# Seven block products for K and V of six token tiles, in a linear attention block with a gated FFN

## The chip, the cores and the metric

The kernel runs on one core of one Trainium2 chip. The metric is the device time of one execution in microseconds (us); before the change the median of three runs is 758.9 us (758.7 to 759.54). The engines have their own in-order instruction queues and wait for each other on semaphores: PE (TensorE, matrix products into PSUM), DVE (VectorE), ACT (ScalarE), POOL (GpSimd) and SP, which here issues most DMAs.

## The reference, cut to what matters

```python
def phi(t): return jnp.where(t > 0, t + 1, jnp.exp(t)) + 1e-6

xn = layernorm(x)                     # x: 2048 tokens x 1024
q, k, v = split(xn @ wqkv)            # 32 heads of 32
pq, pk = phi(q), phi(k)
kv = einsum("bhsd,bhse->bhde", pk, v) # sum over all tokens
z  = einsum("bhsd->bhd", pk)
num, den = pq @ kv, pq . z + 1e-6
s = (num / den) @ wo
g = silu((silu(xn @ w_gate) * (xn @ w_up)) @ w_down)   # width 3584
out = x + s * g
```

All tensors are bfloat16; the normalised tokens are kept in float16.

## The kernel before, in words

The kernel has three stages. The first makes the normalised, transposed tokens, K and V, the sum kv and most of Q; the second makes the attention output s; the third is the FFN with the final combination. The change is in the first two. Their order on PE, DVE, ACT and POOL is written out by hand (FRONT_ORDER): an engine executes what the program emits for it in just that order.

**Tiles and blocks.** The 2048 tokens are 16 tiles of 128, and 4 blocks of 4 tiles. xnT holds the transposed tokens in two tensors of 1024 tokens (pass 0: blocks 0 and 1; pass 1: blocks 2 and 3). Tiles 0 to 7 are normalised one by one and transposed on PE. Blocks 2 and 3 go another way: statistics on DVE (L322, L335), three small Newton steps on POOL for the reciprocal root (L362 to L366), the norm on DVE (emit_norm, L371) into a piece of ws_all, and emit_xT_block: a DMA to DRAM (L415) and a transposing DMA back into xnT (L416), both on SP's queue.

**A K/V tile directly.** emit_B(i, c) computes one of four column chunks of 512 of a token tile: 8 matmuls of 512 columns over the 1024 input features (L428). For the two chunks of K, ACT evaluates exp and relu out of PSUM (L186, L187), and after the second chunk DVE makes phi from them in two operations (L190, L191). The two chunks of V are copied to v_sb by ACT (L446). emit_C(i) then adds the tile's outer products of phi(K) and V into three PSUM tiles kvz (8 matmuls of 129 columns, L457); it needs both copies of V.

**Q by seven block products.** A QGroup computes 256 columns of Q for 1024 tokens as a 2 x 2 block product with seven products instead of eight (a Strassen-Winograd form). Its operands are sums of blocks of xnT (xsum_ops, L138: five operations of 128x2048 per pass) and of the weights (wsum_ops, L152 to L155: four operations per group of 256 columns). Each product is 4 matmuls of 512 columns, so a group has 28 instead of 32. Part a makes two products into accumulators X and Y, ACT copies X to SBUF (L228), DVE adds Y (L231). Part b makes a product into Z, DVE adds it (L236), then one more product each on top of X and Y, which gives two of the four blocks, evaluated by ACT. Part c makes the last two products on top of X and Y; DVE subtracts them from the sum (L246), and ACT evaluates the result. Part d is phi on DVE (L190, L191) for a row of 1024 tokens.

**The order of the first stage.** After the first tiles, a loop over tiles 4 to 15 emits the four chunks of each tile; from tile 9 on, one of six QGroups is interleaved with each tile. Two more (qa, qb) come in the second stage. Between the chunks, fill(n) takes operations from a list, later: statistics, norms, transposes, then the sums for Q. PSUM has five buffers (psB) for the chunks and for X, Y and Z.

**The second stage.** emit_KVZ masks kvz on DVE. emit_ND makes numerator and denominator of one token tile (8 matmuls, L632) and divides on DVE (L636 to L642); emit_OT sends the tile to DRAM and back transposed; emit_S is one of 32 units of the product with wo (8 matmuls of 512 columns, L669, copied by ACT, L673). nd tiles and units alternate, and the phi rows left over from qa and qb lie between them. After the last nd tile the first weights of the FFN are loaded.

Of the kernel before, what the change touches and what calls it, by code (L numbers as in the profile page):

```python
# [21 lines left out]
def kernel(  # L22
# [171 lines left out]
    wqp = p12.enter_context(tc.tile_pool(name="wqp", bufs=1))  # L194
    phiw = p12.enter_context(tc.tile_pool(name="phiw", bufs=5))
    qtmp = p12.enter_context(tc.tile_pool(name="qtmp", bufs=2))

    wq_sb = wqp.tile([P, DC, D], BF16, name="wq_sb")
    NM_Q = D // FW
    pqT_tiles = {}  # L200

    def exp_tile():
        return phiw.tile([P, SP_TOK], BF16, name="e_t", tag="e_t")

    class QGroup:


        def __init__(self, p, m):
            w = wq_sb[:, :, m * FW:(m + 1) * FW]
            self.lhs, self.rhs = block_operands(w, ws_all[:, m // 2, m % 2]), x_operands(p)  # L210
            self.out = wgu.tile([P, 2, SP_TOK], BF16, name="pqT", tag=("wg_sb" if m % 2 == 0 else "wu_sb"))
            pqT_tiles[(p, m)] = self.out
            self.row = {}
# [35 lines left out]
        def part_d(self, i):  # L249
            emit_phi(self.out[:, i, :], self.row[i][:])  # L250

    ET = mybir.EngineType
    FRONT_ORDER = {ET.PE, ET.DVE, ET.Activation, ET.Pool}
    kvz_ps = [psA.tile([P, GPT, NDW], FP32, name=f"kvz{j}", tag="A") for j in range(NJ)]
    with ExitStack() as p1:
# [4 lines left out]
        wkv_sb = wpool.tile([P, DC, 2 * D], BF16, name="wkv_sb")  # L260
        NV = 3
        v_bufs = [wpool.tile([P, G, NDW], BF16, name=f"v_sb{k}") for k in range(NV)]
# [7 lines left out]
        def x_ap(i):  # L270
            return xp_tiles[i // 2][:, i % 2, :]
# [45 lines left out]
        def emit_stats(i, parts=None):  # L317
            if i not in part_stats:
                part_stats[i] = small.tile([P, NSC, nc.vector.BN_STATS_DIM], FP32, name="stats", tag="stats")
            xr = x_ap(i).rearrange("p (c f) -> p c f", f=SCH)  # L320
            for c in (range(NSC) if parts is None else parts):
                nc.vector.bn_stats(out=part_stats[i][:, c, :], in_=xr[:, c, :])  # L322
            if parts is None:
                emit_aggr(i)
# [43 lines left out]
        def emit_norm(i, dst, cols=None):  # L368
# [3 lines left out]
                                           op0=ALU.subtract, op1=ALU.mult)  # L372

# [6 lines left out]
        def xn_blk_slot(b):  # L382
            o = xn_base + (1 - b % 2) * TPB * D
            return ws_flat[:, o:o + TPB * D].rearrange("p (t d) -> p t d", t=TPB).bitcast(FP16)
# [35 lines left out]
        kv_tiles = {}  # L420

        def v_of(i):
            return v_bufs[i % NV]

# [27 lines left out]

        def emit_C(i):
            pk_sb, v_sb = pk_tiles.pop(i), v_of(i)
            for g in range(G):
                j, gi = divmod(g, GPT)
                nc.tensor.matmul(kvz_ps[j][:, gi, 0:P + 1], lhsT=pk_sb[:, g * P:(g + 1) * P],  # L457
                                 rhs=v_sb[:, g, 0:P + 1],
                                 start=(i == 0 and gi == 0), stop=(i == NT - 1),
                                 skip_group_check=True)  # L460
# [10 lines left out]


        later = deque()
        for b in range(2, NB):
            for t in range(TPB):
                later.append(lambda i=b * TPB + t: emit_stats(i, parts=(0,)))
                later.append(lambda i=b * TPB + t: (emit_stats(i, parts=(1,)), emit_aggr(i)))
            later.append(lambda i=b * TPB: emit_rstd(i))
            if b > 2:
                for t in range(TPB):  # L480
                    later.append(lambda b=b, t=t: emit_norm(b * TPB + t, xn_blk_slot(b)[:, t, :]))
                later.append(lambda b=b: emit_xT_block(b))
            else:
                norm_b2 = [lambda b=b, t=t: emit_norm(b * TPB + t, xn_blk_slot(b)[:, t, :]) for t in range(TPB)]
                norm_b2.append(lambda b=b: emit_xT_block(b))

        pos = 2 * TPB + 1 + 4
        later = deque(list(later)[:pos] + norm_b2 + list(later)[pos:])
        later.extend(xsum_ops(0))
        for m in range(NM_Q):  # L490
            later.extend(wsum_ops(wq_sb[:, :, m * FW:(m + 1) * FW], ws_all[:, m // 2, m % 2]))
        later.extend(xsum_ops(1))

        def fill(n):
            for _ in range(min(n, len(later))):
                later.popleft()()

        with tc.manual_schedule(engines=FRONT_ORDER):
# [66 lines left out]

            Q0 = 2 * TPB + 1
            early = deque([(0, m) for m in range(NM_Q)] + [(NPASS - 1, m) for m in range(NM_Q - 2)])
            for i in range(TPB, NT):
                grp = QGroup(*early.popleft()) if i >= Q0 and early else None
                nf = 1 if grp else 2  # L570
                emit_B(i, 0)
                fill(nf)
                emit_C(i - 1)
                if grp:
                    grp.part_a()
                emit_B(i, 1)
                fill(nf)
                if grp:
                    grp.part_b()
                if i == TPB:  # L580
                    emit_T(TPB + 2)
                emit_B(i, 2)
                fill(nf)
                if i == TPB:
                    emit_T(TPB + 3)
                if grp:
                    grp.part_c()
                emit_B(i, 3)
                if grp:
                    grp.part_d(0)  # L590
                    grp.part_d(1)
                fill(nf)
            emit_C(NT - 1)
            assert not later and not early
        gate([x_loads[i] for i in range(first_wave, NT)], marks[("B", 1)], sync=True)
        gate(wq_loads, marks[("B", 3)], sync=True)

    with ExitStack() as p2:
# [90 lines left out]
        with tc.manual_schedule(engines=FRONT_ORDER | {ET.SP}):  # L689

            qa, qb = (QGroup(NPASS - 1, m) for m in (NM_Q - 2, NM_Q - 1))
            for c in range(NCC):
                nc.sync.dma_start(out=wo_sb[:, :, c * CW:(c + 1) * CW], in_=wo_v[:, :, c * CW:(c + 1) * CW])
            emit_KVZ()
            qa.part_a()
            qa.part_b()
            nd_tile()
            qb.part_a()
            emit_OT()
            qa.part_c()  # L700
            nd_tile()
            qa.part_d(0)
            qb.part_b()
            emit_OT()
            nd_tile()
            qb.part_c()
            emit_OT()
            rows = deque(((qa, 1), (qb, 0), (qb, 1)))
            while units:
                if len(units) % 4 != 2:  # L710
                    nd_tile()
                else:
                    for _ in range(min(2, len(rows))):
                        grp, i = rows.popleft()
                        grp.part_d(i)
                if len(units) == 2 * NCC:
                    sum_w(0, 0)
                    sum_w(0, 1)
                s_unit()
                emit_OT()  # L720
    p12.close()
    ps12.close()
# [372 lines left out]
```

## Time and profile before

| what | value |
|---|---|
| median of three runs | 758.9 us |
| the profiled execution | 758.81 us |
| its span, first to last instruction | 757.0 us |
| granted TensorE clock, mean | 0.999 |
| PE busy / DVE / ACT / POOL | 746.9 / 482.1 / 276.5 / 50.9 us |
| K/V matmuls (L428) | 379 ns each in the rows, 24 in a row take 5.18 us |
| first stage ends (last kvz) | at about 166.4 us |
| second stage ends (first FFN matmul) | at 244.09 us |

Matmuls are pipelined, so the duration in a row (379 ns) is longer than the distance between two of them (5.18 / 24 = 0.216 us). A group of rows gives line, engine, operation, output and inputs with shapes, count, then busy time and mean ns of one, then the idle time of the engine just before and what ended it. A row of the timeline gives start and duration in us; several instructions of one kind are merged. A few records of matmuls are missing from the trace, so counts in a window can be a little low.

### The profile page before, as it was taken

How to read it: one execution, taken by the hardware profiler on the slowest of the kernel's cores; microseconds unless marked ns; L12 is line 12 of the kernel's file. 1: busy time of each engine (PE TensorE's matmuls, PEld its weight loads, DVE VectorE, ACT ScalarE, POOL GpSimd, SP SyncE). 2: the span in 40 equal slices, each digit the busy share in tenths (PEclk: the TensorE clock that was granted, in tenths of full speed). 3: DMA queues.
4: the chain of work that ended last, by engine and by line, in shares of the span. 5: the costliest groups of instructions: out<-in, count | busy, mean ns of one | idle time of the engine just before them, and what ended most of it. 6: DMA issues, size and time to landing. Idle time of an engine off the chain costs nothing.

```text
span 757.0 us, 9915 instructions
## 1 busy us (share of the span) xinstructions
PE 746.9 (99%) x3724; PEld 351.7 (46%) x3764; DVE 482.1 (64%) x897; ACT 276.5 (37%) x482; POOL 50.9 (7%) x112
## 2 busy tenths in 40 slices
PE   8999999999999999999999999999999999999997
PEld 4544444444544444444444444444444444444454
DVE  6686666349843577776787777776755744445453
ACT  4444556555223434343433334343443111111111
POOL 3311000000000000000000000000000112222220
PEclk9999999999999999999999999999999999999999
DMA  9606100016899334573354634543869854554200
GB/s 318 223 16 184 40 1 0 1 45 186 237 234 287 115 102 146 165 217 110 93 174 147 202 107 131 170 150 112 298 225 352 299 181 181 181 178 171 96 29 29
DMA packets 127663, 115.98 MB, mean 153 GB/s; under 512 B 29440, under 2 KB 108416, under 8 KB 126336
## 3 DMA queue, kind: packets, MB, share of 16 engines
q1 hardware_dynamic: 122720, 106.58, 44.8%
q10 hardware_dynamic: 4896, 8.78, 3.5%
q8 instruction: 29, 0.48, 0.3%
q14 instruction: 18, 0.15, 0.1%
HBM read 70.52 MB, written 38.54 MB: 144 GB/s over the span
## 4 chain that ended last, share of the span: by engine, by line
PE 95%; DVE 3%; issue 1%; DMA 0%; ACT 0%; DVEq 0%; ACTq 0%
PE X L131 29%; PE Y L131 28%; PE kv_ps L428 14%; PE Z L131 10%; PE s_ps L669 6%; PE qY L131 3%; PE qX L131 3%; PE kvz L457 1%; PE nd_ps L632 1%; DVE o_sb L642 1%; PE qZ L131 1%; DVE stats L322 0%; PE tr_ps L397 0%; DMA xp<-in_A_x_dram 0%; DVE pqT L191 0%
## 5 line engine op out<-in xcount | busy, mean ns | idle before, releaser
L131 PEld LDWEIGHTS <-ws_all 128*128 128x128 bf16 x1420 | 137.8, 98 | 162.6 <-issue 0.2
L758 DVE TENSOR_TENSOR q<-n,Y 128x512 f32<-128x512 f32 x63 | 43.4, 688 | 116.8 <-PE Y L131 105.8
L428 PE MATMUL kv_ps<-wkv_sb,xnT 128*128 128x512 bf16 x496 | 114.2, 379 | 1.2 <-DVE xnT L411 0.5
L131 PEld LDWEIGHTS <-xs 128*128 128x128 bf16 x616 | 58.0, 98 | 63.1
L1028 POOL TENSOR_TENSOR o_out<-y,xres 128x512 bf16<-128x512 f32 x29 | 33.5, 1157 | 652.4 <-DVE y L1027 652.4
L428 PEld LDWEIGHTS <-xnT 128*128 128x128 f16 x512 | 49.3, 98 | 57.6 <-DVE xnT L411 0.7
L131 PE MATMUL Y<-xs,ws_all 128*128 128x512 f16 (+3 forms) x308 | 70.3, 360 | 0.0
L131 PE MATMUL X<-xnT,ws_all 128*128 128x512 f16 (+1 forms) x278 | 70.1, 379 | 0.2
L131 PE MATMUL Z<-xs,ws_all 128*128 128x512 f16 x224 | 57.5, 379 | 0.0
L131 PE MATMUL Y<-xnT,ws_all 128*128 128x512 f16 x224 | 57.5, 379 | 0.0
L131 PE MATMUL X<-xs,ws_all 128*128 128x512 f16 x224 | 57.5, 379 | 0.0
L882 ACT ACTIVATE g<-cg 128x512 bf16<-128x512 f32 x56 | 35.4, 633 | 53.9 <-DVE cg L773 53.9
L764 DVE TENSOR_TENSOR u<-Z,q 128x512 f32<-128x512 f32 x63 | 43.3, 688 | 16.0 <-PE Z L131 15.9
L882 ACT ACTIVATE g<-X 128x512 bf16<-128x512 f32 x28 | 16.7, 598 | 99.3 <-PE X L131 99.2
L754 ACT COPY n<-X 128x512 f32<-128x512 f32 x63 | 37.0, 587 | 28.2 <-PE X L131 27.8
L907 DVE TENSOR_TENSOR ho<-g,up 128x1024 bf16<-128x1024 bf16 x56 | 38.3, 686 | 0.5
L131 PEld LDWEIGHTS <-wg_sb 128*128 128x128 bf16 x224 | 21.9, 98 | 26.6 <-issue 0.3
L673 ACT CAST s_sb<-s_ps 128x512 bf16<-128x512 f32 x32 | 18.4, 587 | 43.4 <-PE s_ps L669 29.5
L131 PEld LDWEIGHTS <-wu_sb 128*128 128x128 bf16 x224 | 21.9, 98 | 26.4
L1027 DVE TENSOR_TENSOR y<-y,s_in 128x512 f32<-128x512 f32 x31 | 21.3, 686 | 20.2 <-ACT y L1021 15.9
L1021 ACT ACTIVATE y<-X 128x512 f32<-128x512 f32 x8 | 4.8, 598 | 69.7 <-PE X L131 61.2
L186 ACT ACTIVATE e_t<-kv_ps 128x512 bf16<-128x512 f32 x32 | 19.2, 600 | 29.6 <-PE kv_ps L428 27.2
(140 smaller groups left out, 1046.1 us busy)
## 6 DMA issues: line engine op xcount, KB each, us to landing
h_dram<-ho SPq DMA_DIRECT2D x56, 256.0 KB, 2.5
wg_sb<-in_B_w_gate_dram SPq DMA_DIRECT2D x14, 512.0 KB, 4.0
wu_sb<-in_B_w_up_dram SPq DMA_DIRECT2D x14, 512.0 KB, 4.0
wdr<-in_B_w_down_dram SPq DMA_DIRECT2D x14, 512.0 KB, 4.0
ws_all<-h_dram SPq DMA_DIRECT2D x4, 1792.0 KB, 8.3
wds_dram<-wdsA SPq DMA_DIRECT2D x14, 384.0 KB, 2.6
hp_a<-h_dram SPq DMA_DIRECT2D x3, 1792.0 KB, 9.0
o_dram<-o_sb ACTq DMA_DIRECT2D x16, 256.0 KB, 3.1
```

The lines of the kernel that those rows point to most:

```text
L131: marks["mm"] = nc.tensor.matmul(acc[:, 0:c1 - c0], lhsT=lhs(k), rhs=rhs(k)[:, c0:c1], start=(first and k == 0), stop=(k == n - 1), skip_g ...
L186: nc.scalar.activation(out=e, in_=t, func=ACT.Exp)
L428: mm = nc.tensor.matmul(kv_ps[:], lhsT=xn_tok_ap(i)[:, dc, :], rhs=wkv_sb[:, dc, c * CW:(c + 1) * CW], start=(dc == 0), stop=(dc == DC - 1))
L669: mm = nc.tensor.matmul(s_ps[:], lhsT=oT[:, c, ttok], rhs=wo_sb[:, c, cc * CW:(cc + 1) * CW], start=(c == 0), stop=(c == G - 1))
L673: nc.scalar.copy(out=s_sb[:, cc * CW:(cc + 1) * CW], in_=s_ps[:])
L754: nc.scalar.copy(out=n[:], in_=self.X[:])
L758: nc.vector.tensor_tensor(out=self.q[:], in0=n[:], in1=self.Y[:], op=ALU.add)
L764: nc.vector.tensor_tensor(out=self.u[:], in0=Z[:], in1=self.q[:], op=ALU.add)
L882: nc.scalar.activation(out=self.g[:, i, j * TB:(j + 1) * TB], in_=src, func=ACT.Silu)
L907: nc.vector.tensor_tensor(out=self.ho[:, i], in0=self.g[:, i], in1=self.up[:, i], op=ALU.mult)
L1027: nc.vector.tensor_tensor(out=t[:], in0=t[:], in1=self.s_in[:, i, cs], op=ALU.mult)
L1028: (nc.vector if last and (i, j) != (0, 0) else nc.gpsimd).tensor_tensor(out=self.o_out[:, i, cs], in0=t[:], in1=self.xres[:, i, cs], op=AL ...
```

## The change

Tiles 9/13, 10/14 and 11/15 no longer go through emit_B. A new class, KVGroup, computes K (or V) of two tiles that lie 512 tokens apart, for all 1024 columns, with seven block products; its operands on the token side are the sums that Q of pass 1 uses anyway, its operands on the weight side are sums of quarters of the K (or V) weights, five operations of 128x2048 for each of K and V (kv_sum_ops). Three of these sums are stored in places that are free by then (quarters of xnT that no later product reads, and the buffers of the last two pqT tiles); two are written over the weights' own quarters. Tile 12 follows tile 8, then twelve groups of Q, K and V in the order of seq. A group's part c and its phi are emitted after the next group's part a. The norms of blocks 2 and 3 move from DVE to ACT as one operation with a scale and a bias per partition; DVE computes that bias (emit_neg_mr). The first part of qa moves into the first stage; its phi rows and those of qb move to units 3, 5, 7 and 9 of the second stage, the nd tiles are spread to unit 19. There are four v buffers instead of three, four exp tiles instead of five, and the blocks' places in ws_all are exchanged.

```diff
-    phiw = p12.enter_context(tc.tile_pool(name="phiw", bufs=5))
+    phiw = p12.enter_context(tc.tile_pool(name="phiw", bufs=4))
...
+        def emit_neg_mr(i):
+            gid = grp_of[i]
+            mv, rstd, tiles = grp_state[gid]
+            n = len(tiles)
+            neg_mr[gid] = small.tile([P, TPB], FP32, name="nmr", tag="nmr")
+            nc.vector.scalar_tensor_tensor(out=neg_mr[gid][:, 0:n], in0=mv[:, 0:n, 0], scalar=-1.0, in1=rstd[:, 0:n],
+                                           op0=ALU.mult, op1=ALU.mult)
+
+        def emit_norm_act(i, dst):
+            mv, rstd, k = ln_state[i]
+            nc.scalar.activation(out=dst, in_=x_ap(i), func=ACT.Identity, bias=neg_mr[grp_of[i]][:, k:k + 1],
+                                 scale=rstd[:, k:k + 1])
...
+        def kv_sum_ops(which, places):
+            w = wkv_sb[:, :, which * D:(which + 1) * D]
+            w11, w12, w21, w22 = w[:, 0:HD, 0:CW], w[:, 0:HD, CW:D], w[:, HD:DC, 0:CW], w[:, HD:DC, CW:D]
+            s1, s5, s2 = places
...
+            return [lambda: tt(out=s1, in0=w11, in1=w22, op=ALU.add), lambda: tt(out=s5, in0=w11, in1=w21, op=ALU.add),
+                    lambda: tt(out=s2, in0=w12, in1=w22, op=ALU.add),
+                    lambda: tt(out=w21, in0=w22, in1=w21, op=ALU.subtract),
+                    lambda: tt(out=w12, in0=w11, in1=w12, op=ALU.subtract)]
...
+            def part_b(self):
+                Z = psB.tile([P, CW], FP32, name="kZ", tag="B")
+                self.mm(Z, "M1", True)
+                nc.vector.tensor_tensor(out=self.u[:], in0=self.u[:], in1=Z[:], op=ALU.add)
+                self.mm(self.X, "M5", False)
+                self.direct(0, 1, self.X)
+                self.mm(self.Y, "M2", False)
+                self.direct(1, 0, self.Y)
...
+        st2, st3, no2, no3, xs0 = stats_ops(NB - 2), stats_ops(NB - 1), norm_ops(NB - 2), norm_ops(NB - 1), xsum_ops(0)
+        later.extend(st2 + st3[:4])
+        later.extend(both(a, b_) for a, b_ in zip([both(no2[0], no2[1])] + no2[2:], st3[4:]))
+        later.extend(xs0[:3])
+        later.extend(both(a, b_) for a, b_ in zip([both(no3[0], no3[1])] + no3[2:], xs0[3:] + ws_ops(0)[:3]))
+        later.extend(ws_ops(0)[3:])
...
+            k_ops = kv_sum_ops(0, (pq_place(NPASS - 1, NM_Q - 2), pq_place(NPASS - 1, NM_Q - 1), x_quarter(0, 0, 1)))
+            v_ops = kv_sum_ops(1, (x_quarter(0, 1, 0), x_quarter(1, 0, 1), x_quarter(1, 1, 0)))
+            for ops in (ws_ops(1), xsum_ops(NPASS - 1), k_ops, v_ops, ws_ops(2), ws_ops(3)):
+                later.extend(ops)
...
+            rest = list(range(TPB, 2 * TPB)) + [b * TPB for b in range(2, NB)]
+            fills = {2 * TPB - 1: (1, 2, 1, 1), 2 * TPB: (2, 2, 1, 1), rest[-1]: (1, 1, 1, 1)}
...
+            seq = [(lambda: QGroup(0, 1), 2, 0), (lambda: K(1), 0, 3), (lambda: V(1), 2, 2), (lambda: QGroup(0, 2), 4, 0),
+                   (lambda: K(2), 2, 0), (lambda: V(2), 2, 0), (lambda: QGroup(0, 3), 0, 0),
+                   (lambda: QGroup(NPASS - 1, 0), 0, 0), (lambda: K(3), 0, 0), (lambda: QGroup(NPASS - 1, 1), 0, 0),
+                   (lambda: V(3), 0, 0), (lambda: QGroup(NPASS - 1, NM_Q - 2), 0, 0)]
+            prev = None
+            for make, fa, fb in seq:
+                grp = make()
+                grp.part_a()
+                fill(fa)
+                if prev:
+                    prev.part_c()
+                    prev.post()
+                else:
+                    emit_C(before)
+                if make is not seq[-1][0]:
+                    grp.part_b()
+                    fill(fb)
+                while ready_C:
+                    emit_C(ready_C.popleft(), last=(not ready_C and make is seq[-1][0]))
+                prev = grp
...
-            rows = deque(((qa, 1), (qb, 0), (qb, 1)))
+            rows = deque((grp, i) for grp in (qa, qb) for i in range(2))
+            nd_at = {1, 2, 4, 6, 8, 10, 11, 12, 14, 15, 16, 18, 19}
+            row_at = {3, 5, 7, 9}
```

KVGroup's parts a and c follow those of QGroup; for V, ACT only copies and DVE subtracts straight into v_sb.

## The prediction

> **What bounds the kernel now.** The page comes first: TensorE (PE) is busy nearly everywhere, at full clock.
>
> ```profile
> PE 746.9 (99%) x3724; PEld 351.7 (46%) x3764; DVE 482.1 (64%) x897; ACT 276.5 (37%) x482; POOL 50.9 (7%) x112
> ...
> PEclk9999999999999999999999999999999999999999
> ```
>
> So a matmul taken out is worth its issue time. The chain that ended last shows 24 of them, the number at stake here:
>
> ```profile
> 23.32 5.18 PE kv_ps L428 x24
> ```
>
> The windows (columns: PE, PEld, DVE, ACT, POOL, clock, DMA) show the rest of the K/V stage and the start of the next:
>
> ```profile
> 92.00:165.00 73.00, 72.63 (x368) 34.53 (x373) 37.94 (x62) 44.35 (x81) 0.00 (x0) 1.00 0.00 1
> 165.00:192.00 27.00, 25.82 (x158) 12.77 (x159) 23.16 (x67) 12.84 (x23) 0.00 (x0) 1.00 0.61 182
> ```
>
> In the first PE loses nothing that can be won; in the second 1.2 us at most, with DVE at 86%. Then I read what one instruction of the moved kinds takes, in the groups by shape:
>
> ```profile
> L138 DVE TENSOR_TENSOR xs<-xnT 128x2048 f16<-128x2048 f16 x10 | 11.8, 1219 | 0.0
> ...
> L371 DVE TENSOR_SCALAR ws_all<-xp,mv,rstd 128x1024 f16<-128x1024 bf16 x15 | 7.4, 540 | 4.8 <-POOL rstd L366 4.7
> ...
> L346 ACT ACTIVATE rstd<-mv,eps_ln 128x1 f32<-128x1 f32 x2 | 0.6, 296 | 3.4 <-DVE mv L335 3.4
> ```
>
> and ACT by width, from the kernel's last stage:
>
> ```profile
> L1021 ACT ACTIVATE y<-y 128x512 f32<-128x512 f32 x1 | 0.6, 632 | 3.5 <-DVE y L810 3.5
> L815 ACT ACTIVATE y<-y 128x128 f32<-128x128 f32 x2 | 0.6, 302 | 1.0 <-DVE y L814 1.0
> ```
>
> The timeline around the first moved norms, tile 5 (its kvz waits for both v copies):
>
> ```profile
> 53.75 0.59 ACT L446 CAST v_sb<-kv_ps 128x512 bf16<-128x512 f32 x1 [0.64 <-PE kv_ps L428]
> ...
> 54.52 0.21 DVE L335 BATCH_NORM_AGGREGATE mv<-stats 128x2 f32<-128x12 f32 x1
> 54.65 1.86 DVE L371 TENSOR_SCALAR ws_all<-xp,mv,rstd 128x1024 f16<-128x1024 bf16 x4
> 55.54 0.59 ACT L446 CAST v_sb<-kv_ps 128x512 bf16<-128x512 f32 x1 [1.20 <-PE kv_ps L428]
> ...
> 57.01 0.63 PE L457 MATMUL kvz<-v_sb,pk_sb 128*128 128x129 bf16 x8
> ```
>
> and around the end of one Q group: subtraction, then phi, on DVE:
>
> ```profile
> 88.41 0.69 DVE L246 TENSOR_TENSOR pqT<-qu,qX 128x512 bf16<-128x512 f32 x1 [2.06 <-PE qX L131]
> ...
> 89.87 0.42 DVE L190 TENSOR_SCALAR e_t<-e_t 128x1024 bf16<-128x1024 bf16 x1
> ...
> 91.64 0.69 DVE L191 TENSOR_TENSOR pqT<-e_t,pqT 128x1024 bf16<-128x1024 bf16 x1 [0.15 <-ACT pqT L187]
> ```
>
> Back to back on DVE, starts lie about 0.09 us closer than durations: 5.76 us for five xs make 1.135 us each; a 128x512 operation counts 0.60, the two rows of phi 2.3 with their waits.
>
> **Matmuls.** Each of six groups (K and V of tiles 9/13, 10/14, 11/15) issues 28 where 32 stood: 24 less, all on the path: -5.18 us.
>
> **Norms on ACT.** DVE loses 8 x 0.54 us; it was not the bound there, so nothing comes back. On ACT, 384 elements cost 0.632 - 0.302 = 0.33 us, so 1024 cost 0.632 + 0.44 = 1.07; the 128x1 row (0.296, one operand per partition) against 0.302 - 0.11 = 0.19 without makes 0.10 per such operand, and the norm has two: 1.27, 1.17 between starts. Bounds 0.96 (operands free) to 1.27.
> In front of them: the first norm waits for the new small operation on DVE at 54.65 plus about 0.2, so starts at 54.87. ACT's order is then norm, v copy, norm, norm, v copy, norm. The second copy ends at 54.87 + 1.17 + 0.48 + 2.34 + 0.59 = 59.45; the second half of tile 5's kvz wants it at 57.25. PE waits 2.2 us. For block 3 the same in tile 6, one step worse: the small operation stands behind phi and one xs sum, which follow the exp that the first wait has delayed (61.6 + 0.65 for exp, then 0.53, 0.61, 1.14, 0.2 = 64.7). The copy ends at 64.7 + 4.6 = 69.3; kvz wants it at 64.38 + 2.2 + 0.24 = 66.8: 2.5 us. Sum +4.7, bounds 3.5 to 5.3.
> The Trainium skill, ScalarE: Activation LUTs, Rules for kernel authors, says to leave adds and multiplies to VectorE, and under What ACT_TABLE_LOAD costs it has 280 ns + 0.833 ns an element with one per-partition operand and 93 ns for the next: 1.23 us, against 1.27 worked out above and DVE's 0.54. By it this term would be +4.5.
>
> **Sums of the weights.** Ten operations of 128x2048 enter DVE's queue, each 1.135 us by the xs row. I follow the queue from the end of tile 12, which stands where tile 9 stood, at 90.8 (times as if nothing had waited before it). Q1 is the Q group that follows it, K1 and V1 are tiles 9/13, Q2 the next Q group. Phi of the group before is done at 92.25, as the last row above shows; then come K's s1 (93.4), Q1's add (94.0), s5 and s2 (96.3). PE has done K1's first part at 97.3. Then DVE has, in the program's order: K1's add (to 98.2), Q1's subtractions and phi (102.1), K1's second add (102.7), K's difference sums w21, w12 (105.0), V's s1 (106.1), V1's add, s5, s2 (109.0), K1's subtractions and phi (112.7), V1's add, V's w21, w12 (115.6), Q2's add, four wq sums at 1.6 (117.8), V1's subtractions and Q2's add (119.6). It never rests in these 22 us. PE's matmuls there are 76 of 0.216 and two kvz sets: 17.3 us from 97.3, 114.6. What it waits for: w21 and w12 before K1's last part 1.1 us, V's s1, s5, s2 1.2, V's w21 and w12 (114.5 plus a weight load, wanted at 111.7) 3.35. It ends at 120.3: +5.65. Bounds, for the seven sums in this stretch: two of phi's 0.42 rows, 0.75, would leave 3.0; two of its 0.69 rows, 1.22, make 6.25. I take the xs row, the same operation at the same size.
> PSUM tiles do not come into it: a group's third accumulator follows the previous group's second add, its successor's first the subtraction, each with some 2 us to spare.
>
> **After that.** A Q or K group is 6.04 us of PE against 4.98 of DVE and 4.7 of ACT, a V group less: no wait, unless phi, which now stands before the next group's second add, takes 2 us longer. The extra copies and adds (0.6 + 4 x 0.6 per group) are in that count. At the end the last two kvz sets have no second part before them: +0.15 (0 to 0.7, one subtraction).
>
> **Moves that I cost at nothing.** Block 3's transpose: write 70.4, transpose 4.3 later as now (68.65 to 72.98), landing 6.1 after: 80.9, wanted by tile 12 at 77.4 + 4.7 = 82.1. Cover 1.2 us. SP has only block 2's pair before it, issued five us earlier; POOL's steps for it, 3.4 us by the wait behind them now, end three us before the norm. Four exp tiles instead of five, four v buffers, the places in xnT and pqT: two groups of phi, matmuls long done. Stage 2: one part of the first Q group less before the first nd, phi rows one per unit; bounds -1.2 (all that the window shows) and +2 (o's transposes, 4.3 us to landing, at the first unit). I take 0. The first gate weights are asked for three units of 1.73 later, 5.2 us; now DVE has their sums at 236.9 for a matmul at 245.95, nine us of cover.
>
> **Sum.** -5.18 + 4.7 + 5.65 + 0.15 = +5.3. The profiled execution took 758.81 (span 757.0, 1.8 around it), the median 758.9: 764.1 us.
>
> **Rivals.** *Only the sums wait* (ACT's copies come in time, because a norm takes under 0.45 us, so that the three ahead of the second copy fit in 1.3 us): -5.18 + 5.65 + 0.15, 759.4. For it: ACT is busy 37%. Against: the order on ACT is fixed, two norms before the copy. *Only the norms wait*, the other side: DVE keeps up between K1 and Q2. Its place is those seven K/V sums; it decides when each takes under 0.33 us, since then the 5.65 is gone: -5.18 + 4.7 + 0.15, 758.5, not slower. Against it: the xs row, same size and width of types. *The change does what it is for*, everything beside PE hidden: 753.8. *More goes wrong*: block 3 lands 3 us late, or stage 2 waits for o: 767.
>
> The Trainium skill, VectorE: DVE Perf Modes, Why tensor_tensor can't do 2×_2P or 4×, gives two results a cycle at most: 2048 at 0.96 GHz make 1.07 us; the 1.219 row agrees, with some start cost; nothing there would make 0.33 possible.
>
> **Chances.** Forecast 0.60 (its own range 761 to 766.5), only sums 0.11, only norms 0.09, all hidden 0.07, worse 0.13. The bounds added up give 758.9 to 767.9; the range 757 to 767.5 reaches under them to the case of the norms alone, and leaves out the hidden case and part of the last. A change under 0.2% (1.5 us) can't be told from none here. Faster: the hidden case and part of "only norms", 0.11; same: the rest of that, only sums, a little of the forecast, 0.19; slower 0.70.
>
> **What would show it.** Waits of kvz for v_sb of some 2 us in tiles 5 and 6; waits of kX and kY for wkv_sb and xnT of 1 to 3 us between K1 and Q2, DVE without idle time there; none later. Wrong if those waits are missing, or if norms show well under 1 us.

## The result, and the profile after

The changed kernel takes 768.1 us, median of six runs (765.4 to 771.0), against 758.9 us before (758.7 to 759.5): 1.0121 times as long, 95% interval 1.0109 to 1.0134. The forecast was 764.1 us with a range of 757.0 to 767.5. Slower was right; the time lies 0.6 us above the range and 4 us above the forecast. The profiled execution took 766.83 us, its span is 765.06 us against 757.02: 8.0 us to explain.

The head of its page. PE has 23 records fewer, 24 matmuls less but for the records that a trace lacks, and yet its busy time is nearly the same, 746.1 us for 746.9. The clock looks full in all slices, as before; but a slice is 19 us long, and the digit 9 stands for 90% and more:

```profile
PE 746.1 (98%) x3701; PEld 350.5 (46%) x3740; DVE 504.9 (66%) x925; ACT 283.4 (37%) x490; POOL 55.8 (7%) x113
...
PEclk9999999999999999999999999999999999999999
```

The windows (length, then PE, PEld, DVE, ACT, POOL, clock, DMA share, GB/s), two of them those shown of the kernel before. From 92 to 165 us PE was busy 72.63 us before and 68.25 now, DVE 37.94 before and 57.19 now; from 62 to 92 the mean granted clock is 0.94, from 120 to 130 it is 0.83:

```profile
62.00:92.00 30.00, 27.31 (x134) 12.73 (x136) 15.39 (x25) 15.86 (x26) 2.63 (x6) 0.94 0.49 136
92.00:165.00 73.00, 68.25 (x330) 31.01 (x333) 57.19 (x89) 41.78 (x78) 0.00 (x0) 0.98 0.00 1
165.00:192.00 27.00, 25.76 (x152) 12.97 (x153) 21.30 (x51) 17.25 (x33) 0.00 (x0) 1.00 0.39 117
110.00:120.00 10.00, 7.22 (x29) 2.48 (x28) 9.52 (x13) 4.13 (x9) 0.00 (x0) 1.00 0.00 1
120.00:130.00 10.00, 8.29 (x42) 3.96 (x44) 6.83 (x11) 3.00 (x7) 0.00 (x0) 0.83 0.01 2
```

What PE waits for between 25 and 260 us (engine and what it waited for: us in total, times, the longest):

```profile
PE kvz L486 <- ACT v_sb L475: 4.6, 4, 2.4
PE kX L131 <- DVE wkv_sb L514: 3.4, 2, 2.8
PE s_ps L826 <- DMA oT<-o_dram: 1.1, 1, 1.1
PE kX L131 <- DVE xnT L512: 0.7, 1, 0.7
```

These are the predicted waits: V's copies in tiles 5 and 6, then the weight sums between K1 and Q2. But they add up to 9.8 us, of which the matmuls give back 5.2, and the kernel is 8.0 slower. What is missing shows in the chain that ended last: before, 24 matmuls took 5.18 us; here 31 take 8.38, where 31 x 0.216 would be 6.7, and a group of four takes 1.61 where the groups beside it take 1.03:

```profile
23.63 5.18 PE kv_ps L457 x24
...
70.20 8.38 PE kv_ps L457 x31
...
121.66 1.61 PE kX L131 x4
```

So in two stretches TensorE runs at half its pace. Windows whose borders lie where the granted clock changes: two windows at 0.50, each 3.42 us long; the window right ahead of each, in which PE was busy for 1.05 and 0.60 of 3.41 us; and, first, the one around tile 5's wait, 1.52 us busy, which no drop follows:

```profile
57.12:60.53 3.41, 1.52 (x14) 0.92 (x13) 3.27 (x7) 3.41 (x4) 1.88 (x2) 1.00 0.00 0
67.36:70.77 3.41, 1.05 (x10) 0.61 (x8) 1.78 (x5) 3.41 (x4) 0.00 (x0) 1.00 1.24 277
70.77:74.19 3.42, 3.42 (x10) 1.19 (x9) 0.50 (x2) 2.18 (x5) 0.00 (x0) 0.50 0.73 267
118.56:121.97 3.41, 0.60 (x4) 0.20 (x3) 3.26 (x6) 2.03 (x4) 0.00 (x0) 1.00 0.01 2
121.97:125.39 3.42, 3.42 (x10) 1.18 (x9) 3.42 (x7) 0.00 (x0) 0.00 (x0) 0.50 0.02 5
```

In such a stretch matmuls of 512 columns start 0.427 us apart instead of 0.216; eight of them stand where sixteen would, so each stretch costs 1.7 us. All borders lie on one grid: from 74.19 to 121.97 is 14 x 3.413 us.

**The account of the span**, from distances between starts of matmuls, after less before:

| place | us |
|---|---|
| up to the first kvz (28.34, now 28.64) | +0.3 |
| 24 matmuls less | -5.2 |
| kvz of tiles 5 and 6 for v_sb | +4.9 |
| K1, V1 for the weight sums | +5.4 |
| two stretches at half clock | +3.4 |
| small gaps of the first stage, less those of before | 0.0 |
| second stage (75.4 us; before 77.9, 1.7 of it now in the first stage) | -0.7 |
| FFN, 512.85 for 512.93 | -0.1 |
| sum | +8.0 |

The small gaps are what remains to the first stage's own difference of 8.5 us (first to last kvz 148.1 for 137.9, less the 1.7 us of qa's first part).

### The profile page after: what moved, and what is told of

It is laid out like the page before. It is cut to its first block, busy times and chain, and to the rows that moved or that the text cites. A ratio compares the mean times of both kernels' runs of the same rounds, so it can differ in the third digit from the quotient of the medians.

```text
span 765.1 us, 9919 instructions
## 1 busy us (share of the span) xinstructions
PE 746.1 (98%) x3701; PEld 350.5 (46%) x3740; DVE 504.9 (66%) x925; ACT 283.4 (37%) x490; POOL 55.8 (7%) x113
## 4 chain that ended last, share of the span: by engine, by line
PE 89%; DVE 4%; ACT 2%; DMA 2%; issue 1%; POOL 1%; DVEq 0%; ACTq 0%
PE X L131 28%; PE Y L131 28%; PE Z L131 9%; PE kv_ps L457 7%; PE s_ps L826 6%; PE qX L131 2%; PE qY L131 2%; PE kY L131 1%; PE kX L131 1%; DMA o_dram<-o_sb 1%; PE kvz L486 1%; ACT e_t L186 1%; DMA oT<-o_dram 1%; PE qZ L131 1%; PE nd_ps L789 1%
## 5 line engine op out<-in xcount | busy, mean ns | idle before, releaser
L131 PEld LDWEIGHTS <-ws_all 128*128 128x128 bf16 x1420 | 137.9, 98 | 162.6 <-issue 0.9
L131 PEld LDWEIGHTS <-xs 128*128 128x128 bf16 (+1 forms) x736 | 69.6, 98 | 82.7 <-DVE wkv_sb L514 4.4
L1188 POOL TENSOR_TENSOR o_out<-y,xres 128x512 bf16<-128x512 f32 x29 | 35.2, 1213 | 660.4 <-DVE y L1187 660.4
L457 PE MATMUL kv_ps<-wkv_sb,xnT 128*128 128x512 bf16 x311 | 73.1, 385 | 0.9 <-DVE xnT L436 0.5
L457 PEld LDWEIGHTS <-xnT 128*128 128x128 f16 x320 | 30.9, 99 | 36.5 <-issue 2.4
L826 PE MATMUL s_ps<-wo_sb,oT 128*128 128x512 bf16 x124 | 29.0, 379 | 1.4 <-DMA oT<-o_dram 1.1
```

The lines of the kernel that those rows point to most:

```text
L131: marks["mm"] = nc.tensor.matmul(acc[:, 0:c1 - c0], lhsT=lhs(k), rhs=rhs(k)[:, c0:c1], start=(first and k == 0), stop=(k == n - 1), skip_g ...
L457: mm = nc.tensor.matmul(kv_ps[:], lhsT=xn_tok_ap(i)[:, dc, :], rhs=wkv_sb[:, dc, c * CW:(c + 1) * CW], start=(dc == 0), stop=(dc == DC - 1))
L826: mm = nc.tensor.matmul(s_ps[:], lhsT=oT[:, c, ttok], rhs=wo_sb[:, c, cc * CW:(cc + 1) * CW], start=(c == 0), stop=(c == G - 1))
L1188: (nc.vector if last and (i, j) != (0, 0) else nc.gpsimd).tensor_tensor(out=self.o_out[:, i, cs], in0=t[:], in1=self.xres[:, i, cs], op=AL ...
```

## The experiments

The theory: (a) two norms ahead of V's second copy in ACT's queue make the waits of kvz; (b) the weight sums, all emitted in one place, make DVE late between K1 and Q2; (c) an idle stretch of TensorE costs more than its length, because the clock halves after it. The rivals stand in the expectations.

All kernels below replace the 18 transposing DMAs by plain DMAs of the same bytes, so the tokens of blocks 2 and 3 and o are not transposed and the outputs are not the reference's. Only their times are used. The two controls show what that does to the time.

| kernel | median us (runs) | against the kernel before, 95% |
|---|---|---|
| c_before | 758.8 (758.5 to 759.6) | 0.9998, 0.9989 to 1.0006 |
| c_after | 767.1 (765.2 to 768.5) | 1.0102, 1.0088 to 1.0117 |
| p1_norms_dve | 764.4 (764.0 to 764.5) | 1.0067, 1.0054 to 1.0080 |
| p2_no_kv_sums | 760.1 (758.4 to 760.9) | 1.0012, 1.0004 to 1.0021 |
| p4_keep_warm | 767.5 (766.8 to 768.3) | 1.0115, 1.0101 to 1.0129 |
| p5_keep_warm | 764.5 (763.4 to 766.0) | 1.0079, 1.0065 to 1.0093 |
| g1_act_spread | 761.8 (761.3 to 763.1) | 1.0043, 1.0030 to 1.0057 |
| p3_pool_sums | 767.7 (767.3 to 770.4) | 1.0124, 1.0109 to 1.0139 |
| g3_both_dve | 757.2 (756.5 to 757.9) | 0.9977, 0.9968 to 0.9987 |
| g4_both_dve | 756.3 (755.3 to 757.8) | 0.9965, 0.9953 to 0.9978 |
| g5_nd_first | 755.2 (754.7 to 755.6) | 0.9949, 0.9937 to 0.9962 |
| g6_nd_first | 755.1 (754.9 to 756.1) | 0.9951, 0.9937 to 0.9964 |

### The two controls

```diff
-            nc.sync.dma_start_transpose(out=xn_blk_ap(b), in_=blk_rows(xn_dram, b))
+            nc.sync.dma_start(out=xn_blk_ap(b), in_=blk_rows(xn_dram, b).rearrange("(p a) (h t) -> p (a h) t", p=P, t=TB))
...
-                nc.sync.dma_start_transpose(out=oT_of(b)[:, :, t * P:(t + 1) * P], in_=o_dram[r0:r0 + P, :])
+                nc.sync.dma_start(out=oT_of(b)[:, :, t * P:(t + 1) * P], in_=o_dram[r0:r0 + P, :].rearrange("p (g t) -> p g t", t=P))
```

> Control for the runs that follow: the changed kernel with its 18 transposing DMAs (blocks 2 and 3 of the tokens, and o) replaced by plain DMAs of the same bytes between the same tensors, so what is computed from them is not the reference's; all else stays. Theory (the waits are made by ACT's order, by DVE's backlog and by the clock after them, not by these DMAs): the same waits of kvz and kX as in the changed kernel and two stretches with matmuls 0.427 us apart; only the wait of s_ps for o, 1.1 us, may go: 766 to 769 us. Rival (the transposing DMAs come late in some executions, which is why its runs spread from 765.4 to 771.0): the runs agree within 1 us, and the median falls to about 765.

> Control: the kernel before with its 18 transposing DMAs replaced by plain ones of the same bytes (the tokens of blocks 2 and 3 and o are then not transposed). Theory: they are hidden, but for up to 1.2 us of waits at the start of the second stage: 757.7 to 759.2 us, no stretch at half pace after the start.

Measured: 767.1 and 758.8 us. c_after has the same waits to 0.1 us and two stretches at half clock, at 70.83 and 122.03 us; its runs spread over 3.3 us, those of the changed kernel over 5.6. So the transposing DMAs do not make the loss, nor all of the spread, and the difference of 8.3 us between the controls can stand for the change's 9.2; the 0.9 us between them are within the runs' spread. The wait of s_ps stayed too, at 1.2 us.

### The norms back on DVE

```diff
-            ops = [lambda i=b * TPB + t, t=t: emit_norm_act(i, xn_blk_slot(b)[:, t, :]) for t in range(TPB)]
-            return [lambda: emit_neg_mr(b * TPB)] + ops + [lambda: emit_xT_block(b)]
+            ops = [lambda i=b * TPB + t, t=t: emit_norm(i, xn_blk_slot(b)[:, t, :]) for t in range(TPB)]
+            return [lambda: None] + ops + [lambda: emit_xT_block(b)]
```

> As c_after, with the eight norms of blocks 2 and 3 back on DVE, at the same places of the list. Theory (the norms delay V's copies in ACT's queue): the waits of kvz for v_sb in tiles 5 and 6, 4.6 us together, are gone, and with the second of them the stretch at half pace from 70.8 to 74.2 us (1.8 us). The waits between K1 and Q2 stay. 6.4 us under c_after (4.5 to 7). Rival (the copies are late for another reason, such as two operations taken from the list at once): the waits of kvz stay above 2 us, and the time is within 2 us of c_after.

Measured: 2.7 us under c_after, not 6.4. Its waits of PE:

```profile
PE kX L131 <- DVE wkv_sb L514: 3.4, 2, 2.8
PE kvz L486 <- DVE pk_sb L191: 1.8, 1, 1.8
PE kv_ps L457 <- DMA xnT<-xn_dram: 1.7, 1, 1.7
```

The waits for v_sb and the first stretch at half clock are gone, as (a) and (c) say. Two waits that had been covered came up in their place: phi of K now stands behind norms and sums in DVE's queue, where DVE itself first waits 2.05 us for POOL's rstd, and tile 12, no longer held up, waits 1.7 us for block 3. By starts the two are 3.6 us, about the 3.7 that were missing. So on DVE, too, the norms make PE wait from these places of the list.

### Without the weight sums

```diff
-            kv_rhs[which] = {"M4": lambda k: w22[:, k, :], "M3": lambda k: w11[:, k, :], "M1": lambda k: s1[:, k, :],
+            kv_rhs[which] = {"M4": lambda k: w22[:, k, :], "M3": lambda k: w11[:, k, :], "M1": lambda k: w11[:, k, :],
...
-                             "M5": lambda k: s5[:, k, :], "M2": lambda k: s2[:, k, :],
+                             "M5": lambda k: w21[:, k, :], "M2": lambda k: w12[:, k, :],
...
-            return [lambda: tt(out=s1, in0=w11, in1=w22, op=ALU.add), lambda: tt(out=s5, in0=w11, in1=w21, op=ALU.add),
...
+            return [lambda: None] * 5
```

> As c_after, without the ten sums of K's and V's weights: the products read quarters of the weights as they are, so K and V of six tiles are not the reference's; all matmuls stay. Theory (DVE's backlog between K1 and Q2 is made by these sums): the waits of kX for wkv_sb and xnT, 5.4 us by the distances between matmuls, are gone, and with them the stretch at half pace from 122.0 to 125.4 us (1.8 us): 7.2 us under c_after (5 to 7.5). Rival (DVE is late there because of phi and the adds of two groups in a row): less than 2 us comes back.

Measured: 7.0 us under c_after, where 7.2 was expected. PE waits for nothing between K1 and Q2, and there is no stretch at half clock there; the first one, after tile 6's wait, stays. Its waits of PE:

```profile
PE kvz L486 <- ACT v_sb L475: 4.6, 4, 2.4
PE s_ps L822 <- DMA oT<-o_dram: 2.3, 2, 1.4
```

That is (b): without these ten operations phi and the adds keep up.

### The clock alone

Small matmuls fill a part of each wait; the waits end when ACT or DVE is done, so only the idle time changes.

```diff
+    def keep_warm(n):
+        for _ in range(n):
+            nc.tensor.matmul(spare, lhsT=warm[:, 0:P], rhs=warm[:, 0:512 - GPT * NDW], start=False, stop=False,
+                             skip_group_check=True)
...
                 fill(nf[0])
+                if i == TPB + 2:
+                    keep_warm(30)
+                if i == TPB + 3:
+                    keep_warm(34)
                 emit_C(before)
...
                 if prev:
+                    if isinstance(prev, KVGroup) and prev.which == 1 and prev.tiles[0] % TPB == 1:
+                        keep_warm(40)
                     prev.part_c()
```

> As c_after, with small matmuls (zeros, 116 columns, into unused columns of a PSUM tile) put ahead of the three long waits: 20 in tile 6 and 32 in tile 7 ahead of kvz, 40 ahead of V1's part c. At 0.056 us each they fill 1.1, 1.8 and 2.2 us of waits of 2.1, 2.5 and 3.0. Theory (the granted clock halves when TensorE has been idle for most of a stretch of 3.41 us): the waits end when they ended, no stretch shows matmuls 0.427 us apart, the median falls by 3.4 us from c_after's 767.1 to 763.6 (763 to 764.5), and the runs agree within 1 us. Rival (the half pace has another cause than idle time): the two stretches stay, 767 us or more, up to 5 us more where the small matmuls do not fit into the waits.

> p4_keep_warm with its small matmuls at the right places: 30 ahead of tile 5's kvz (1.7 of the 2.1 us that it waits), 34 ahead of tile 6's (1.9 of 2.7), 40 ahead of V1's part c (2.2 of 3.0). Theory (TensorE's clock halves for 3.41 us when it was idle for more than about 60% of the 3.41 us before): no stretch at half pace in any run, the waits end where they ended, and the median falls by the two stretches, 2 x 1.7 us, from c_after's 767.1 to 763.7 (763.0 to 764.5). Rival (the stretches cost nothing, since DVE and ACT, which make the next waits, are not slowed by them): the stretches go, but the time stays above 766.

p4 had the first two groups one tile too early, so 20 matmuls (1.1 us) stood before a kvz that waits for nothing, and tile 6's wait of 2.4 us stayed empty. It measured 767.5 us. Its profile is a test all the same: after the wait that stayed empty the clock halved, at 70.80 us, after the filled one ahead of V1's part c it did not.

p5, with the right places, measured 764.5 us, 2.5 under c_after where 3.4 was expected. Its profiled execution has no stretch at half clock. The windows on its grid that lie over the ends of the three waits now hold PE for 3.00, 2.59 and 2.63 us:

```profile
58.59:62.01 3.42, 3.00 (x23) 1.63 (x22) 1.97 (x2) 3.32 (x6) 2.93 (x7) 1.00 0.17 65
...
68.83:72.25 3.42, 2.59 (x15) 1.34 (x16) 0.11 (x1) 3.33 (x6) 0.00 (x0) 1.00 0.48 167
...
116.62:120.03 3.41, 2.63 (x43) 2.23 (x43) 3.26 (x6) 2.08 (x4) 0.00 (x0) 1.00 0.01 2
```

One profile shows one execution, but the mean granted clock is known for every run: 0.998 to 1.000 in the five of p5, 0.994 to 0.997 in the five of c_after, and one stretch of 3.41 us at half clock lowers it by 0.002. So the half pace is made by idle time, and its cost reaches the end of the kernel, against the rival that ACT and DVE would take it up. Of the 3.4 us expected, 0.9 did not come back; p5's runs spread over 2.6 us, and why is open. 764.5 us is also near what the prediction's own terms give, 764.1, waits counted at their length and no drop of the clock.

### The order on ACT

```diff
-        later.extend(st2 + st3[:4])
-        later.extend(both(a, b_) for a, b_ in zip([both(no2[0], no2[1])] + no2[2:], st3[4:]))
-        later.extend(xs0[:3])
-        later.extend(both(a, b_) for a, b_ in zip([both(no3[0], no3[1])] + no3[2:], xs0[3:] + ws_ops(0)[:3]))
-        later.extend(ws_ops(0)[3:])
+        w0 = ws_ops(0)
+        later.extend(st2 + st3[:2] + [both(st3[2], no2[0])])
+        for n in range(3):
+            later.extend([both(no2[1 + n], st3[3 + 2 * n]), st3[4 + 2 * n]])
+        later.extend([both(no2[4], no2[5]), no3[0]])
+        for n in range(3):
+            later.extend([no3[1 + n], xs0[n]])
+        later.extend([both(no3[4], no3[5]), xs0[3], xs0[4], w0[0], both(w0[1], w0[2]), w0[3]])
```

Tile 7 takes two operations in each of its first three places and none in the last.

> As c_after, with the norms still on ACT, but at most one in each place between two chunks, so that no two stand ahead of V's second copy, and the sums of pass 0 behind block 3's small operation. Theory (the order on ACT, not the length of a norm, made the waits of kvz): the waits for v_sb fall under 0.5 us each, the first stretch at half pace is gone, tile 12 may wait up to 1 us for block 3: 767.1 - 6 = 761 us (760 to 763). Rival (ACT has no room for norms of 1.24 us in tiles 5 to 7 whatever their order): waits of kvz of 2 us and more stay, 765 us or more.

Measured: 761.8 us, 5.3 under c_after. The norms are as long as before (in the changed kernel 1239 ns for 128x1024), and there are as many of them on ACT; only the order of the list differs, for ACT and for DVE, and of the 4.6 us 0.5 remain:

```profile
PE kvz L486 <- ACT v_sb L475: 0.5, 2, 0.4
PE kv_ps L457 <- DMA xnT<-xn_dram: 0.3, 1, 0.3
```

The second line is the price: with PE no longer late, block 3 has no cover left. How the order on ACT made the waits is seen in ACT's timeline of the changed kernel (start, duration): one norm, the copy, two norms, the copy.

```profile
55.08 1.24 ACT L396 ACTIVATE ws_all<-xp,nmr,rstd 128x1024 f16<-128x1024 bf16 x1 [1.68 <-DVE nmr L391]
56.23 0.56 ACT L475 CAST v_sb<-kv_ps 128x512 bf16<-128x512 f32 x1
56.69 2.37 ACT L396 ACTIVATE ws_all<-xp,nmr,rstd 128x1024 f16<-128x1024 bf16 x2
58.97 0.56 ACT L475 CAST v_sb<-kv_ps 128x512 bf16<-128x512 f32 x1
```

PE's second half of kvz starts when that copy is done:

```profile
57.30 0.40 PE L486 MATMUL kvz<-v_sb,pk_sb 128*128 128x129 bf16 x4
59.59 0.39 PE L486 MATMUL kvz<-v_sb,pk_sb 128*128 128x129 bf16 x4 [1.89 <-ACT v_sb L475]
```

In tile 6 the order on DVE has a part as well. Block 3's small operation waits there for the last of twelve steps on POOL, which run beside DVE's xs sums in the changed kernel and are held up by them:

```profile
58.57 1.10 POOL L371 TENSOR_TENSOR lnw<-rstd 128x4 f32<-128x4 f32 x1 [5.71 <-DVE rstd L366]
59.75 1.06 POOL L372 TENSOR_TENSOR lnw<-lnw,lna 128x4 f32<-128x4 f32 x1
...
64.86 0.20 POOL L375 TENSOR_TENSOR rstd<-rstd,lnw 128x4 f32<-128x4 f32 x1
```

They take 6.5 us, and the chain that ended last runs through them. In g1, where these sums come after the small operation, each step takes 0.20 us and all twelve 3.3. How much of the gain in tile 6 comes from this and how much from the order on ACT was not taken apart.

### K's sums on POOL

```diff
+            tp = nc.gpsimd.tensor_tensor
+            if which == 0:
+                return [lambda: tp(out=s1, in0=w11, in1=w22, op=ALU.add), lambda: tp(out=s5, in0=w11, in1=w21, op=ALU.add),
...
+            pool_ops.extend(k_ops)
-            for ops in (ws_ops(1), xsum_ops(NPASS - 1), k_ops, v_ops, ws_ops(2), ws_ops(3)):
+            for ops in (ws_ops(1), xsum_ops(NPASS - 1), v_ops, ws_ops(2), ws_ops(3)):
```

> As c_after, with K's five weight sums on POOL, idle from 62 to 178 us: s1, s5, s2 from tile 8 on, w21 and w12 after tile 12's K chunks; V's five stay on DVE and come earlier by the places that K's leave. From POOL's row of 128x512 (1.213 us) a sum of 128x2048 is estimated at 4.9 us: K's would end at about 102 us, wanted at 104 and 110. Theory: DVE has 5.7 us less between 90 and 110, the waits between K1 and Q2 fall below 1 us and their half pace goes: 767.1 - 6.5 = 760.6 us, 759 to 762.5. Rival (POOL and DVE hinder each other where DVE does sums: POOL's small steps took 1.1 us instead of 0.20 beside xs): K's sums come late, kX waits for wkv_sb as long as before or longer, 767 us or more.

Measured: 767.7 us, nothing gained. The rival is right in kind but not in place: kX waits for no sum, K's are early enough. But operations of DVE with two inputs in SBUF stand still while POOL adds; one with an input in PSUM, at 92.25, took its usual 0.69 us beside a sum. Two sums on POOL took 9.12 us, about as estimated:

```profile
64.87 9.12 POOL L514 TENSOR_TENSOR pqT<-wkv_sb 128x2048 bf16<-128x2048 bf16 x2
```

In that time DVE's small operation on four numbers a partition, 0.17 us in c_after, took 4.02, and two xs sums 6.21 instead of 2.35:

```profile
64.92 4.02 DVE L391 SCALAR_TENSOR_TENSOR nmr<-mv,rstd 128x4 f32<-128x4 f32 x1 [0.37 <-POOL rstd L375]
68.87 6.21 DVE L138 TENSOR_TENSOR xs<-xnT 128x2048 f16<-128x2048 f16 x2
```

So the norms of block 3 came 3.7 us later, and PE's waits for v_sb rose from 4.6 to 10.6 us. The clock was at half for two windows in a row, 6.83 us.

### Both orders, on DVE alone

DVE of c_after rests for 4.4 us before 73.6 and 5.9 us before 81.7. g3 puts four of the ten sums there:

```diff
-            for ops in (ws_ops(1), xsum_ops(NPASS - 1), k_ops, v_ops, ws_ops(2), ws_ops(3)):
+            for ops in (k_ops[:2], ws_ops(1), k_ops[2:3], v_ops[:1], xsum_ops(NPASS - 1), v_ops[1:3], k_ops[3:], v_ops[3:],
+                        ws_ops(2), ws_ops(3)):
```

Tiles 8 and 12 take (2, 2, 2, 2) and (2, 2, 2, 1) operations, and seq's counts for V1 and Q2 are smaller by the sums that moved; the rest as g1.

> As g1_act_spread, and four of the ten weight sums (K's s1, s5, s2, V's s1) go into tile 8, where DVE was idle for 5.9 us, V's s5 and s2 into tile 12, the four in place directly behind. Theory (the sums are only badly placed: DVE has room for them before K1): no wait of kX over 0.5 us, no stretch at half pace: 758.8 (c_before) - 5.2 (24 matmuls) + up to 1.5 of small waits = 753.6 to 755.1 us, faster than the kernel before. Rival (DVE is short of time from tile 8 to Q2 as a whole, so the backlog only moves to tile 12 or to phi of the first Q group): waits of 3 us or more elsewhere, 757 us or more.

Measured: 757.2 us, faster than the kernel before, but 2 us short of the expectation. There is no half pace; two waits of PE remained, 1.2 us in tile 12 for a sum that stood one chunk too early, and 1.1 us ahead of V1's part c for V's direct copies, behind K1's exp and relu on ACT, which wait for DVE. g4 moves these:

```diff
-            for ops in (k_ops[:2], ws_ops(1), k_ops[2:3], v_ops[:1], xsum_ops(NPASS - 1), v_ops[1:3], k_ops[3:], v_ops[3:],
+            for ops in (k_ops[:2], ws_ops(1), k_ops[2:3], v_ops[:1], xsum_ops(NPASS - 1), [v_ops[2], v_ops[1]], k_ops[3:], v_ops[3:],
...
                     prev.part_c()
+                    fill(behind)
                     prev.post()
```

behind is a fourth count in seq, 2 for K1, so V's w21 and w12 stand between K1's subtractions and its phi.

> g3_both_dve, corrected: V's s5, whose place is a quarter of xnT that tile 12's last chunk still reads, comes after that chunk (there PE waited 1.2 us for it, and read the sum in place of tokens); and V's w21 and w12 stand behind K1's subtractions, the sums for Q2 behind V1's second add. Theory: the waits of 1.4 us in tile 12 and of 1.25 us ahead of V1's part c go: 757.2 - 2.6 = 754.6 us (753.8 to 755.5), faster than the kernel before by 0.5%. Rival (DVE's queue from 85 to 116 us is full whatever its order, so each sum that is moved back delays phi or a subtraction): a wait of 1 us or more at another place between K1 and K2, 756 us or more.

Measured: 756.3 us, 0.9965 of the kernel before (0.9953 to 0.9978). Expected was 754.6. The wait ahead of V1's part c is gone, though Q2 now waits 0.2 us for its moved sums. The wait for the sum in tile 12 only gave way to one of 0.9 us right behind, where the tile's kvz waits for V's second copy, on an ACT that waits for DVE. Theory and rival both hold in part: DVE has room for all ten sums, and little more. Its waits of PE:

```profile
PE kvz L486 <- ACT v_sb L475: 1.5, 3, 0.9
PE s_ps L833 <- DMA oT<-o_dram: 1.3, 1, 1.3
```

### An nd tile ahead of the first unit

```diff
-            nd_at = {1, 2, 4, 6, 8, 10, 11, 12, 14, 15, 16, 18, 19}
+            nd_at = {0, 1, 2, 4, 6, 10, 11, 12, 14, 15, 16, 18, 19}
```

g5 left out 19 instead of 8, so that one nd tile came ahead of a phi row that it reads.

> g4_both_dve, and one nd tile ahead of the first unit of the second stage, where s_ps waits 1.3 us for the first transposed o in all runs with the changed order; the last one (unit 19) goes for it. Theory: its 8 matmuls, some 0.5 us, fill the wait: 0.5 us under g4_both_dve. Rival (nd waits there for DVE to free its PSUM tiles, as in the kernel before, 0.3 to 0.4 us twice): within 0.2 us of g4_both_dve, or slower.

> g5_nd_first with the nd tile taken from unit 8 instead of unit 19: there tile 8 of the tokens came before the last phi row that it reads. Theory: the nd tile ahead of unit 0 fills 0.5 us of the wait of s_ps for the first transposed o, nothing new waits: 755.2 to 755.9 us, 0.5 under g4_both_dve and as much as g5_nd_first. Rival (three nd tiles at units 10 to 12 in a row after a gap make DVE, or the transposes of o behind them, late): 756.5 us or more.

Measured: 755.2 and 755.1 us. The wait of s_ps falls from 1.3 to 0.8 and 0.7 us, as expected; the spans of the profiled executions are 752.9 and 753.2 against 753.5, so of the 1.2 us between the medians only 0.3 to 0.6 is shown. 0.9949 (g5) and 0.9951 (g6) of the kernel before are the best ratios measured; they do not differ from each other, nor, within the intervals, from g4's 0.9965. With the transposing DMAs none of the corrected orders was run, and that g6's order leaves the values as g4 has them is not shown.

## Why the prediction was right or wrong

**The step that failed** is the sum itself: it counts each wait of PE at its own length ("2.2 us", "2.5 us", "3.35"), as if matmuls after it ran at 0.216 us. No term and no rival has the granted clock, which the profile before showed at full everywhere; PE's longest wait there was 1.2 us, at the start. The two longest waits each led to 3.41 us at half clock, 1.7 us each. With that term the forecast would have been 767.5. p4 and p5 show the cause, p5 with 764.5 us.

**The matmuls**, -5.18: in the account to 0.2 us, and g4 and g6, with most waits gone, are faster than the control c_before by 2.5 and 3.6 us of them; beside the 2.7 that g4 lacks stand waits of 3.2 us in its profile, against 0.9 in c_before's.

**The norms on ACT**, +4.7: right in size, and in part by luck. 1239 ns each against 1.27 us, waits of 2.1 and 2.5 us and 0.3 for the first copies against 2.2 and 2.5. The stated order, two norms ahead of the second copy, stands in ACT's timeline, and with the other order of g1 the waits are gone. But for tile 6 the prediction has the small operation behind phi and one xs sum, ready at 64.7; it waited 0.37 us longer, for POOL. POOL's steps were said to end three us before the norm; slowed by the xs sums, they ended 0.2 us before it.

**The sums**, +5.65: right, 5.4. K1's last part waited 1.3 us in all (1.1 predicted), V1 for s1, s5, s2 1.1 (1.2), for w21 and w12 3.0 (3.35). p2 shows the cause.

**The moves costed at nothing.** Stage 2 is 0.7 us shorter, inside its bounds, though s_ps waits 1.1 us for the first o; the FFN is unchanged. Block 3's transpose was given 1.2 us of cover; in the changed kernel it had more, because PE was late. In g1, where PE is not, tile 12 waits 0.3 us, though with plain DMAs and another order of the norms: that suggests that the cover was about as thin as said, and that the norms' waits hid it.

**The rivals.** Only sums (759.4), only norms (758.5) and all hidden (753.8) have their conditions excluded by the rows: a norm at 1.24 us, a sum at 1.22. "More goes wrong", 767 us, has the time nearly, but for reasons that did not occur: block 3 was not late, and o's transposes cost nothing net.

**What stays open.** The changed kernel's runs spread over 5.6 us, those of the kernel before over 0.9. The half clock does not explain it: the mean granted clock is 0.994 to 0.996 in all six, and the shortest run, 765.4 us, and the longest, 771.0, both have 0.996. p5, whose profile has no half pace, also spreads over 2.6 us, and only one execution of each kernel has a trace. What the spread comes from, and why the median lies 1.3 us above the profiled execution, was not found.

## What to carry to other kernels

Price a wait of TensorE at its length, and when it can leave TensorE busy for less than a third of a window of 3.41 us, add 1.7 us; so two short waits can be cheaper than one long. When an operation moves to another engine, look at which instruction stands next in that engine's queue and who waits for it, not at the engine's share: here ACT was 37% busy, and a change of the list's order alone won back 5.3 us. Work that makes an engine late in one place may be free 20 us earlier: four of ten sums, moved into DVE's own rests, together with that order turned 1.0% slower (c_after) into 0.35% faster (g4), in kernels with plain DMAs.

## What the runs showed of the hardware

**The clock after idle time.** The granted clock falls to 0.50 for a window of 3.41 to 3.42 us, and all changes in an execution lie on one grid of 3.413 us. Each window on the grid in which PE was busy for 1.06 us or less was followed by a drop: 1.05 and 0.60 in the changed kernel, 1.06 and 0.60 in c_after, 0.80 in p1, 0.97 in p2, 0.89 in p4, 0.90 in g1, 0.0 and then 0.88 in p3. None followed the windows of 1.52 and more: 1.52 in the changed kernel, c_after and p3, 1.59 and 2.08 in p1, 1.63 in p2, 1.74 in p4. So the limit lies between 31% and 45% busy, and whether a wait of 2 to 3 us costs 1.7 us more should depend on where it falls on the grid. The runs of p2, whose longest wait before the second stage is tile 6's 2.4 us, fit this: three of its eleven, 758.4 to 759.5 us, have a mean clock of 0.999 or 1.000, the other eight, 759.9 to 760.9 us, one of 0.996 to 0.998. A window and the drop behind it, in g1, with the same wait for the sums as in c_after:

```profile
113.20:116.61 3.41, 0.90 (x4) 0.31 (x4) 3.38 (x4) 1.44 (x3) 0.00 (x0) 1.00 0.00 0
116.61:120.03 3.42, 3.32 (x9) 1.19 (x9) 3.42 (x8) 0.00 (x0) 0.00 (x0) 0.50 0.02 5
```

The Trainium skill, TensorE: Matmul & The Clock Gate, What's actually happening, has the half clock, the window of 3413 ns and that it runs free; the runs agree. Its table has the drop after one idle window of about 3.4 us, and under Why this matters for your kernels it warns of gaps over about 3 us; by that, the wait of 2.35 us ahead of 70.77 would have cost nothing more. By the measurement, which decides, a window need not be idle throughout.

**POOL and DVE.** A sum of 128x2048 on POOL took 4.05 to 5.11 us in p3, 3.3 to 4.2 times DVE's 1.22, and held up DVE operations with two inputs in SBUF that started beside it until it ended: 4.02 us for a small one. It also goes the other way: the sum of 5.11 us started beside an xs sum of 1.21 us, and POOL's small steps, 0.20 us each, took 1.10 and 1.06 beside DVE's xs sums in the changed kernel.

The Trainium skill, SBUF — State Buffer, SBUF: two separate sides, says that a GpSimd operation and a DVE operation with two SBUF inputs lock each other out for the whole instruction; p3 agrees.
